# Wk read as plain rows and turned on TensorE at the start of a fused attention and gated-MLP layer

## The chip, the cores and the metric

The kernel runs on one core of a Trainium2 chip. The time is device microseconds of one execution, given as the median of several runs. A second figure is the span of the profiled execution, from its first to its last instruction. TensorE (PE) multiplies matrices into PSUM; VectorE (DVE), ScalarE (ACT) and GpSimd (POOL) do the rest of the arithmetic; SyncE (SP) and ACT issue the transfers (DMA), each through a queue of its own.

## The reference, cut to what matters

x is 2048 x 640, in bf16. The layer has 32 heads of 20 features.

```python
def _A_ref(x, wqkv, w_phi, wo):                 # x: layer-normed rows
    qkv = x @ wqkv                              # 640 -> 3 * 640, split into q, k, v of 32 heads
    pq = einsum("bhsd,hdf->bhsf", q, w_phi)     # a 20 x 20 map per head
    pk = einsum("bhsd,hdf->bhsf", k, w_phi)
    phi_q = concatenate([softmax(pq), softmax(-pq)])
    phi_k = concatenate([softmax(pk), softmax(-pk)])
    kv = einsum("bhsf,bhsd->bhfd", phi_k, v)    # summed over all rows
    z  = einsum("bhsf->bhf", phi_k)
    num = einsum("bhqf,bhfd->bhqd", phi_q, kv)
    den = einsum("bhqf,bhf->bhq", phi_q, z) + 1e-6
    return (num / den) @ wo
h  = x + _A_ref(layernorm(x), wqkv, w_phi, wo)
h2 = h + ((n @ w_gate) * (n @ w_up)) @ w_down   # n = layernorm(h), 640 -> 1536 -> 640
```

## The kernel before, in words

The 2048 rows are cut into 16 tiles of 128 (t = 0 to 15), the 640 features into 5 chunks of 128. The kernel writes its work down as a list of operations with what each reads and writes (`build_graph`). A scheduler, `schedule`, walks that list with a table of planned costs and decides the order on each engine; a program then emits each engine's list with the waits that the reads and writes need. The table `TUNED` (lines 47 to 134) holds, for each operation by name, a key by which the scheduler picks among the operations that are ready, and after a second colon which of several engines does it (0, or nothing, is the first). Every engine works through its list strictly in that order. So the order on the chip comes from `TUNED`, not from the order of the lines.

The stages, by the names that the operations have:

- **Folding the feature map into the weights.** k is needed only as pk, so the kernel multiplies the 20 x 20 maps into Wk once: F1_i, i = 0 to 4 (line 375, function `fold`), six small products for each chunk of 128 rows of Wk. A product takes its stationary operand with the contraction along the partitions, so the fold needs Wk transposed (`wkT`, kept in the buffer `scratch`). Before, wkT comes straight from memory by five transposing loads, wk0 to wk4 (line 282, on SP's queue). The other operand is Phi (line 356: Ph0, Ph1, Ph2), the small maps (w5, from memory) times a 0/1 pattern GL that POOL makes (lines 318 to 337). Fe1_i copies a folded chunk from PSUM to `Wp` (line 237, a helper `copy` used by all evacuations). The same is done for Wq later (F0_i, with transposing loads wqt).
- **Layer norm of x.** x tiles arrive by plain loads (line 272, names x0, x1, x2, x4 and so on; x2 brings tiles 2 and 3, x4 tiles 4 and 5, x6 tiles 6 and 7). Per tile DVE computes statistics (L1s, lines 392 and 393; L1a, line 395), ACT the reciprocal deviation in two steps (L1l and L1e, lines 400 and 403), and DVE or ACT the normed tile xn (lines 428 and 426).
- **Turning x.** Tiles 0 to 3 are transposed on TensorE against an identity matrix, xt0 to xt3 (line 437, five transposes of 128 columns each), and copied to `xnT` by xte0 to xte3 (line 237). Tiles 4 to 15 are turned by transposing transfers from SP (line 446).
- **K and V of each tile** (line 459): V_t from the weights loaded by wv0, wv2, wv4 (line 272), K_t from the folded Wk. Ten products of 320 columns each, evacuated as Ve_t and as two exponentials Kx (line 480); then sums (line 483), reciprocal, scaling on POOL (line 488), and the product KV_t (line 497) that adds up kv and z over the tiles. For tiles 0 and 1 the ten products are five operations of two each, K0_0 to K0_4 and so on, so that each can start when its chunk of weights is there.
- **Q** (line 518), the numerator (551), normalising, the output product with Wo (594), a second layer norm, the gated MLP (636 and 655) and the result (667, 669). The change touches these only through the order.

At the start, before any data is there, TensorE multiplies zeros: 14 products of 512 columns, warm0 to warm13 (line 347). Their result is not used.

The graph of before lists the start of the queues in this form:

```python
xload("sp", 0, 1, -100)
for i in range(NC):
    G.op("sp", "wk%d" % i, lambda e, i=i: e.dma_start_transpose(
        out=T["wkT"][:, :, P * i:P * (i + 1)],
        in_=T["A_wqkv"][P * i:P * (i + 1), D:2 * D]), 1.22, 2.6, [], [wkt_b[i]], key=-99 + i, dma=-1)
xload("act", 1, 2, -95, also=["sp"])
```

With the keys of before SP issues: x0, w5, wk1, wv4, wk2, wk0, x6, wk3, x4, wk4, x8; ACT issues x1, wv0, x2, wv2. TensorE's order is: 14 zero products, xt1, xt0, V1_0, V1_1, F1_1, then sixteen products of V0 and V1, F1_0, F1_2, xt3, xt2, F1_3, K1 and K0, F1_4 and so on.

Of the kernel before, what the change touches and what calls it, by code (L numbers as in the profile page):

```python
# [59 lines left out]
xn9:29.307 xt9:29.987 xn10:29.235:1 xt10:31.207 xn11:36.578:1 xt11:40.017 xn12:43.657:1 xt12:45.087 xn13:42.944:1 xt13:43.867 xn14:45.139 xt14:46.307  # L60
xn15:46.099 xt15:47.527 V0_0:8.987 V0_1:10.074 V0_2:10.345 V0_3:10.617 V0_4:10.889 Ve0:11.43 K0_0:13.51 K0_1:13.782 K0_2:14.054 K0_3:14.325 K0_4:17.085
Kx0_0:18.422 Kx0_1:20.292 Ks0:21.347 Kr0:24.047 Kn0:25.766 KV0:29.582 V1_0:8.129 V1_1:8.4 V1_2:9.259 V1_3:9.53 V1_4:9.802 Ve1:10.344:1 K1_0:12.887
K1_1:13.159 K1_2:14.912 K1_3:15.184 K1_4:16.814 Kx1_0:17.799 Kx1_1:19.045 Ks1:19.927 Kr1:22.767 Kn1:23.407 KV1:31.616 V2:18.715 Ve2:21.539 K2:17.357
Kx2_0:19.669 Kx2_1:20.915 Ks2:25.437 Kr2:28.387 Kn2:29.085 KV2:32.292 V3:15.455 Ve3:17.455:1 K3:20.074 Kx3_0:22.162 Kx3_1:22.995 Ks3:29.807 Kr3:32.047
Kn3:33.803 KV3:37.043 V4:21.432 Ve4:23.619 K4:22.79 Kx4_0:24.419 Kx4_1:25.252 Ks4:26.967 Kr4:28.847 Kn4:31.444 KV4:37.719 V5:32.968 Ve5:34.597
K5:30.258 Kx5_0:32.562 Kx5_1:33.396 Ks5:36.747 Kr5:38.987 Kn5:39.627 KV5:42.47 V6:26.865 Ve6:28.494 K6:28.224 Kx6_0:30.528 Kx6_1:31.361 Ks6:34.257
Kr6:36.177 Kn6:36.817 KV6:43.146 V7:25.507 Ve7:27.552 K7:24.149 Kx7_0:25.875 Kx7_1:26.709 Ks7:39.557 Kr7:42.507 Kn7:43.22 KV7:46.854 V8:41.112
Ve8:42.967:1 K8:39.754 Kx8_0:41.487 Kx8_1:42.32 Ks8:43.719 Kr8:45.639 Kn8:46.279 KV8:48.888 V9:35.685 Ve9:37.915 K9:34.327 Kx9_0:35.955 Kx9_1:37.292
Ks9:41.087 Kr9:46.599 Kn9:48.638 KV9:52.281 V10:38.395 Ve10:40.024 K10:44.137 Kx10_0:45.766 Kx10_1:46.599 Ks10:47.432 Kr10:50.309 Kn10:50.997
KV10:55.674 V11:54.315 Ve11:55.944:1 K11:45.496 Kx11_0:47.222 Kx11_1:48.056 Ks11:48.889 Kr11:50.769 Kn11:53.356 KV11:60.74 V12:57.708 Ve12:59.336  # L70
K12:49.564 Kx12_0:51.193 Kx12_1:52.026 Ks12:53.506 Kr12:55.106 Kn12:58.074 KV12:61.416 V13:50.923 Ve13:52.649 K13:47.53 Kx13_0:49.158 Kx13_1:49.992
Ks13:51.229 Kr13:52.829 Kn13:55.715 KV13:62.722 V14:56.35 Ve14:58.115:1 K14:52.957 Kx14_0:54.585 Kx14_1:55.419 Ks14:56.695 Kr14:58.867 Kn14:60.433
KV14:63.398 V15:64.389 Ve15:66.017:1 K15:59.066 Kx15_0:60.695 Kx15_1:61.528 Ks15:62.361 Kr15:63.961 Kn15:64.601 KV15:68.985 KVe0:69.931 KVe1:70.541
KVe2:71.151 F0_0:60.425 Fe0_0:61.01:1 F0_1:62.407 Fe0_1:63.3 F0_2:62.092 Fe0_2:62.677 F0_3:43.822 Fe0_3:44.407 F0_4:64.074 Fe0_4:64.659 Q0_0:66.826
Qx0_0_0:68.692 Qx0_0_1:68.175 Q0_1:65.747 Qx0_1_0:67.096 Qx0_1_1:67.613 Q0_2:70.74 Qx0_2_0:72.089 Qx0_2_1:72.606 Q0_3:67.905 Qx0_3_0:69.255
Qx0_3_1:69.771 Q0_4:69.661 Qx0_4_0:71.526 Qx0_4_1:71.01 Q1_0:73.933 Qx1_0_0:75.799 Qx1_0_1:75.282 Q1_1:90.247 Qx1_1_0:91.596 Qx1_1_1:92.113 Q1_2:75.012
Qx1_2_0:76.878 Qx1_2_1:76.361 Q1_3:79.676 Qx1_3_0:81.541 Qx1_3_1:81.025 Q1_4:89.168 Qx1_4_0:90.517 Qx1_4_1:91.034 Q2_0:77.172 Qx2_0_0:79.038
Qx2_0_1:78.521 Q2_1:78.596 Qx2_1_0:79.946 Qx2_1_1:80.462 Q2_2:92.751 Qx2_2_0:94.616 Qx2_2_1:94.1 Q2_3:87.744 Qx2_3_0:89.61 Qx2_3_1:89.093 Q2_4:84.961
Qx2_4_0:86.827 Qx2_4_1:86.311 Q3_0:76.093 Qx3_0_0:77.442 Qx3_0_1:77.959 Q3_1:80.755 Qx3_1_0:82.104 Qx3_1_1:82.621 Q3_2:71.819 Qx3_2_0:73.168
Qx3_2_1:73.685 Q3_3:82.524 Qx3_3_0:83.873 Qx3_3_1:84.39 Q3_4:91.326 Qx3_4_0:92.676 Qx3_4_1:93.192 wd0:96.76 wd1:95.06 wd2:94.1 wd3:94.58 N0_1:73.588  # L80
N0_0:72.898 sr0:74.203 rho0:74.693 A0:75.063 B0:76.093 dd0:77.123 rd0:77.513 o0:77.993:1 oT0:78.905 O0:83.603 h0:85.231 L2s0:86.833 L2a0:87.863
L2v0:88.153 L2r0:90.306 hc0:88.153 hT0:89.076 N1_1:78.251 N1_0:73.243 sr1:78.866 rho1:79.356 A1:79.726 B1:80.756 dd1:81.786 rd1:82.176 o1:82.656:1
oT1:83.568 O1:86.386 h1:88.014 L2s1:89.066 L2a1:90.196 L2v1:90.517 L2r1:91.976 hc1:90.626:1 hT1:91.887 N2_1:88.823 N2_0:86.041 sr2:89.886 rho2:90.436
A2:91.126 B2:92.156 dd2:93.186 rd2:93.576 o2:94.056 oT2:95.54 O2:102.227 h2:103.856 L2s2:104.817 L2a2:105.937 L2v2:107.388 L2r2:107.816 hc2:106.399:1
# [131 lines left out]
def mm_c(*ns):  # L216
    return sum(max(0.028, n / 2400.0 + 0.0025) for n in ns)
# [798 lines left out]
```

## Time and profile before

| | |
|---|---|
| median of 5 runs | 283.04 us (282.42 to 283.19) |
| the profiled execution | 283.04 us, span 281.3 us |
| instructions | 4981 |
| granted TensorE clock | 1.000 over the span |
| transfers | 21.98 MB, mean 78 GB/s |

How to read the profile: busy time is the time in which an engine has an instruction in it. A group of instructions of one line is shown with its start, its busy time, what it writes and reads, how many they are, and in brackets how long the engine was idle before and who released it. "PE" is the product on TensorE, "PEld" the loading of its stationary operand, which runs beside it. "SPq" and "ACTq" are issues of transfers. The chain of waits follows the work that ended last back to the start, at each step to what released it.

The busy tenths of TensorE over 40 slices of 7 us:

```profile
PE   6799999999999999999999999999999999999996
```

### The profile page before, as it was taken

Reading aid. Unit: us, or ns where it says so; the run is one execution under the profiler, and the core shown is the slowest. Engines: PE = TensorE matmul, PEld = TensorE weight load, DVE = VectorE, ACT = ScalarE, POOL = GpSimd, SP = SyncE. Lnnn points to the kernel's source line nnn. Section 1 sums busy time; section 2 is a strip of 40 time slices with the busy share of each in tenths; the row PEclk is TensorE's granted clock in tenths of the full one; section 3 lists DMA queues with packets and bytes.
Section 4 is the critical chain, followed back from the end, with each engine's and each line's share of the span. In section 5 each row is a group of like instructions: output and inputs, shape, how many; then the busy total and the mean of one; then the engine's idle time right before and its main releaser. Section 6 shows DMA issues by size and latency. Waiting matters only on the chain.

```text
span 281.3 us, 4981 instructions
## 1 busy us (share of the span) xinstructions
PE 274.0 (97%) x2038; PEld 181.6 (65%) x2054; DVE 181.1 (64%) x370; ACT 102.0 (36%) x182; POOL 60.9 (22%) x77
## 2 busy tenths in 40 slices
PE   6799999999999999999999999999999999999996
PEld 2577878787556689775455664456677454667884
DVE  4799998964488779898577880338793144343242
ACT  2598768545795742113123012211201023230210
POOL 6015997993001222222001000001200000000000
DMA  7937943891012593155202131000236001000002
GB/s 151 265 79 156 154 102 75 249 393 73 0 23 26 121 273 75 26 117 68 51 0 49 23 77 42 0 24 3 50 78 106 24 0 26 1 2 23 29 23 67
DMA packets 46151, 21.98 MB, mean 78 GB/s; under 512 B 37936, under 2 KB 44848, under 8 KB 46128
## 3 DMA queue, kind: packets, MB, share of 16 engines
q1 hardware_dynamic: 45168, 20.52, 32.5%
q10 hardware_dynamic: 960, 1.15, 1.6%
q8 instruction: 16, 0.26, 0.4%
q14 instruction: 7, 0.06, 0.1%
HBM read 10.18 MB, written 2.62 MB: 46 GB/s over the span
## 4 chain that ended last, share of the span: by engine, by line
PE 95%; DMA 3%; issue 0%; SPq 0%; DVE 0%; DVEq 0%
PE ps L636 37%; PE ps L655 19%; PE ps L459 15%; PE ps L594 8%; PE ps L518 8%; PE ps L551 4%; PE ps L497 4%; DMA scratch<-in_A_wqkv_dram 3%; PE ps L375 1%; SPq L272 0%; PE ps L437 0%; DVE Wp L667 0%; DVEq L954 0%
## 5 line engine op out<-in xcount | busy, mean ns | idle before, releaser
L636 PE MATMUL ps<-xnT,Wgu 128*128 128x512 bf16 (+1 forms) x588 | 105.7, 335 | 0.6
L636 PEld LDWEIGHTS ps<-xnT,Wgu 128*128 128x128 bf16 x600 | 58.3, 98 | 43.0 <-DVE ev L644 0.4
L641 ACT ACTIVATE scratch<-ps 128x512 bf16<-128x512 f32 (+1 forms) x60 | 30.6, 511 | 110.6 <-PE ps L636 107.0
L644 DVE TENSOR_TENSOR ev<-ps,scratch 128x512 bf16<-128x512 f32 (+1 forms) x60 | 33.3, 575 | 36.3 <-PE ps L636 19.5
L655 PE MATMUL ps<-Wp,ev 128*128 128x320 bf16 (+2 forms) x396 | 54.0, 295 | 0.0
L655 PEld LDWEIGHTS ps<-Wp,ev 128*128 128x128 bf16 x396 | 38.1, 98 | 14.1
L459 PE MATMUL ps<-Wp,xnT 128*128 128x320 bf16 x320 | 45.6, 299 | 0.4 <-ACT xnT L237 0.4
L488 POOL TENSOR_TENSOR ev<-ev,SR 128x1280 bf16<-128x1280 bf16 x16 | 37.3, 2356 | 8.3 <-DVE SR L486 8.1
L459 PEld LDWEIGHTS ps<-Wp,xnT 128*128 128x128 bf16 x320 | 30.7, 98 | 11.8 <-issue 0.5
L667 DVE SCALAR_TENSOR_TENSOR Wp<-ps,rs,x_all 128x640 bf16<-128x640 f32 (+3 forms) x18 | 14.6, 809 | 25.4 <-PE ps L655 25.2
L583 POOL TENSOR_TENSOR scratch<-scratch,sm 128x640 bf16<-128x640 f32 x10 | 12.7, 1271 | 57.4 <-DVE sm L580 43.6
L527 ACT ACTIVATE eqT<-ps 128x512 bf16<-128x512 f32 x40 | 21.6, 595 | 7.0 <-PE ps L518 7.0
L594 PE MATMUL ps<-Wo,scratch 128*128 128x320 bf16 x160 | 24.2, 299 | 0.0
L483 DVE TENSOR_REDUCE SR<-ev 128x64 f32<-128x1280 bf16 x16 | 23.4, 1475 | 0.7 <-ACT ev L480 0.5
L480 ACT ACTIVATE ev<-ps 128x640 bf16<-128x640 f32 x32 | 20.8, 705 | 7.3 <-PE ps L459 5.9
L608 POOL TENSOR_SCALAR ln<-mv 128x1 f32<-128x1 f32 x16 | 3.3, 209 | 89.0 <-DVE mv L607 77.4
L518 PE MATMUL ps<-xnT,Wp 128*128 128x512 bf16 x96 | 22.3, 379 | 0.2
L598 DVE TENSOR_TENSOR x_all<-ps,x_all 128x640 bf16<-128x640 f32 x16 | 13.2, 822 | 13.0 <-PE ps L594 13.0
L594 PEld LDWEIGHTS ps<-Wo,scratch 128*128 128x128 bf16 x160 | 15.5, 98 | 6.4
L617 ACT ACTIVATE xn<-x_all,mv 128x640 bf16<-128x640 bf16 x9 | 7.4, 825 | 26.1 <-DVE mv L607 26.0
L518 PEld LDWEIGHTS ps<-xnT,Wp 128*128 128x128 bf16 x100 | 9.6, 98 | 9.9 <-DVE KVm L504 0.2
L551 PE MATMUL ps<-KVm,eqT 128*128 128x154 bf16 (+1 forms) x192 | 15.4, 221 | 0.0
(53 smaller groups left out, 202.4 us busy)
## 6 DMA issues: line engine op xcount, KB each, us to landing
out_dram<-Wp SPq DMA_DIRECT2D x15, 160.0 KB, 1.8
x_all<-in_A_x_dram SPq DMA_DIRECT2D x6, 320.0 KB, 3.5
Wgu<-in_B_w_up_dram SPq DMA_DIRECT2D x5, 384.0 KB, 10.1
Wgu<-in_B_w_gate_dram SPq DMA_DIRECT2D x5, 384.0 KB, 6.8
Wp<-in_B_w_down_dram SPq DMA_DIRECT2D x4, 480.0 KB, 5.4
Wp<-in_A_wqkv_dram ACTq DMA_DIRECT2D x2, 320.0 KB, 6.7
Wo<-in_A_wo_dram SPq DMA_DIRECT2D x1, 480.0 KB, 8.5
xnT<-xn SPq DMA_TRANSPOSE x28, 2.6
```

What stands on the lines that cost most here:

```text
L459: ins = e.matmul(pb(b, hb)[:, 0:320], lhsT=T["xnT"][:, NC - 1 - c, P * t:P * (t + 1)], rhs=T["Wp"][:, kind, c, 320 * hb:320 * (hb + 1)], s ...
L480: G.op("act", "Kx%d_%d" % (t, s), lambda e, s=s, b=b, ek=ek: e.activation(out=T["ek"][:, ek.slots[0], s, :].rearrange("p (b n) -> p b n", ...
L483: G.op("dve", "Ks%d" % t, lambda e, ek=ek, sr=sr: e.tensor_reduce(out=T["SR"][:, sr.slots[0], 0, :], in_=T["ek"][:, ek.slots[0], :, :].rea ...
L488: G.op("pool", "Kn%d" % t, lambda e, ek=ek, sr=sr: e.tensor_tensor(out=T["ek"][:, ek.slots[0], :, :].rearrange("p s (h f) -> p (s h) f", f ...
L518: ins = e.matmul(pb(b)[:, 0:n], lhsT=T["Wp"][:, 0, i, P * c:P * (c + 1)], rhs=T["xnT"][:, NC - 1 - i, o0:o0 + n], start=(i == 0), stop=(i ...
L527: G.op("act", "Qx%d_%d_%d" % (q, c, s), lambda e, s=s, c=c, o0=o0, n=n, b=b: e.activation(out=T["eqT"][:, s, c, o0:o0 + n], in_=pb(b)[:, 0 ...
L551: ins = e.matmul(pb(b, y)[:, 22 * h0:22 * (h0 + j1 - j0)], lhsT=T["eqT"][:, s, c, P * t:P * (t + 1)], rhs=T["KVm"][:, OFF[s, c] + j0:OFF[s ...
L594: ins = e.matmul(pb(b, hb)[:, 0:320], lhsT=T["oT"][:, oT.slots[0], c, :], rhs=T["Wo"][:, c, 320 * hb:320 * (hb + 1)], start=(c == 0), stop ...
L636: ins = e.matmul(pb(b)[:, 0:n], lhsT=T["Wgu"][:, gu, c, P * ft:P * (ft + 1)], rhs=T["xnT"][:, NC - 1 - c, o0:o0 + n], start=(c == 0), stop ...
L641: G.op("act", "g%d_%d" % (bi, ft), lambda e, pg=pg, gt=gt, n=n: e.activation(out=T["gt"][:, gt.slots[0], 0:n], in_=pb(pg)[:, 0:n], func=AF ...
L644: o_ = G.op("dve", "u%d_%d" % (bi, ft), lambda e, pu=pu, gt=gt, hh=hh, ft=ft, n=n: e.tensor_tensor(out=T["hh"][:, hh.slots[0], ft, 0:n], i ...
L655: ins = e.matmul(pb(b, hb)[:, 0:w], lhsT=T["hh"][:, hh.slots[0], ft, P * tt:P * (tt + 1)], rhs=T["Wd"][:, ft, c0 + w * hb:c0 + w * (hb + 1 ...
```

## The change: what it does

1. Wk is loaded as plain rows into a new view `wkn` of the scratch buffer: wk0 (rows of chunks 0 and 1), wk2 (chunks 2 and 3), wk4 (chunk 4). Each may go on SP's or on ACT's queue.
2. Each of the five chunks is transposed on TensorE, WT0 to WT4: five transposes of 128 columns against the identity, into one PSUM bank; WTe0 to WTe4 copy the bank to `wkT`. Nothing else that reads `wkT` is changed.
3. The planner's rate for plain loads is written anew, and the whole table `TUNED` is replaced, so the order of every engine is another.

The diff, without the rest of the table:

```diff
-x0:0.7 wk0:4.58 wk1:1.66 wk2:3.36 wk3:6.28 wk4:7.98 x1:0.7 wv0:1.18 wv2:2.14 wv4:2.88:1 x2:1.66 x4:7.5 x6:5.8 w5:1.18 x8:9.2 x10:19.229 x12:26.289
...
+x0:0.7 wk0:1.18:1 wk2:1.66:1 wk4:2.14 x1:0.7 wv0:2.14 wv2:2.62:1 wv4:3.1:1 x2:1.66:1 x4:3.58 x6:2.62:1 w5:1.18 x8:4.06 x10:22.303 x12:22.783 x14:19.383
...
+    wkn_b = [Buf("wkn%d" % i) for i in range(NC)]
     wkt_b = [Buf("wkt%d" % i) for i in range(NC)]
...
     xload("sp", 0, 1, -100)
-    for i in range(NC):
-        G.op("sp", "wk%d" % i, lambda e, i=i: e.dma_start_transpose(
-            out=T["wkT"][:, :, P * i:P * (i + 1)],
-            in_=T["A_wqkv"][P * i:P * (i + 1), D:2 * D]), 1.22, 2.6, [], [wkt_b[i]], key=-99 + i, dma=-1)
+    for n_, (a, b_) in enumerate(((0, 2), (2, 4), (4, 5))):
+        dma("sp", "wk%d" % a, lambda a=a, b_=b_: T["wkn"][:, a:b_, :],
+            lambda a=a, b_=b_: T["A_wqkv"][P * a:P * b_, D:2 * D].rearrange("(c p) n -> p c n", p=P), 164 * (b_ - a),
+            wkn_b[a:b_], key=-99 + n_, also=["act"])
...
+    for i in range(NC):
+        b = Buf("pwt%d" % i, "psum")
+        def wt(e, i=i, b=b):
+            for c in range(NC):
+                ins = e.transpose(out=pb(b).bitcast(BF16)[:, P * c:P * (c + 1)], in_=T["wkn"][:, i, P * c:P * (c + 1)],
+                                  identity=T["ident"][:, :])
+            return ins
+        G.op("pe", "WT%d" % i, wt, mm_c(*[P] * NC), LT, [wkn_b[i], id_b], [b], -90 + i)
+        evac("WTe%d" % i, lambda e, eng, i=i, b=b: copy(
+            e, eng, T["wkT"][:, :, P * i:P * (i + 1)], pb(b).bitcast(BF16)[:, 0:D].rearrange("p (c n) -> p c n", c=NC)),
+             640, [b], [wkt_b[i]], -90 + i, i % 2, 320)
...
-                bw += o.dma / (190.0 if bw < 6.2 else 368.0)
+                bw += o.dma / (300.0 if bw < 4.5 else 200.0 if bw < 7.5 else 368.0)
...
-        sc = sb([P, max(nsc, 2 * NC * D)], BF16, "scratch")
+        sc = sb([P, max(nsc, 3 * NC * D)], BF16, "scratch")
...
+        T["wkn"] = sc[:, 2 * NC * D:3 * NC * D].rearrange("p (c n) -> p c n", c=NC)
```

The order that the new table gives at the start:

- SP issues x0, w5, x2, wk4, wv2, wv4, x4, x8, and then the first transposing transfers of x tiles. ACT issues x1, wk0, wk2, wv0, x6.
- TensorE: nine zero products, WT1, WT0, five zero products, F1_1, F1_0, WT2, xt0, xt1, WT3, F1_2, K0_0 and K0_1, F1_3, V1_0 and K0_2, WT4, V1_1, K0_3, V0_0 and V0_1, F1_4, the rest of V1, of V0, xt2, K0_4, xt3, the first of K1, K2, V2, V3 and so on.
- ACT: two L1l, WTe1, two L1e, Fe1_1, Fe1_0, xte1, Fe1_2, Fe1_3, WTe4, L1l and L1e of tiles 2 and 3, Fe1_4.
- DVE: the statistics of tiles 1 and 0, Ph1 and Ph2, WTe0, xn0 and xn1, WTe2, xte0, WTe3, the statistics of tiles 2 and 3, those of tiles 6 and 7, then xn2 and xn3.
- POOL: the constant of `va` first, the identity, then the pattern GL, eps, Ph0.

Over the rest of the kernel the operations are the same, in another order; POOL scales fewer of the tiles' numerators (line 583) and DVE more.

## The prediction

> **What bounds the kernel now.** I read the page's busy table first, then the chain of waits in order of time, then TensorE's timeline, then the transfers of the first 15 us.
>
> ```profile
> PE 274.0 (97%) x2038; PEld 181.6 (65%) x2054; DVE 181.1 (64%) x370; ACT 102.0 (36%) x182; POOL 60.9 (22%) x77
> ...
> 1.71 8.43 DMA scratch<-in_A_wqkv_dram
> 10.15 0.05 issue
> 10.19 0.49 PE ps L375 x6
> ...
> 269.09 9.82 PE ps L655 x84
> 278.92 0.03 issue
> ```
>
> The chain is TensorE's own work from 10.19 us to 278.92; nothing but breaks of 0.05 us stands between its pieces. Before 10.19 it is one transfer, a transposing load of Wk (scratch is where it lands), issued at 1.71 and on chip at 10.15. So the change can gain only ahead of 10.19, and whatever it adds to TensorE counts in full.
>
> ```profile
> 1.24 4.53 PE L347 MATMUL ps<-zero 128*128 128x512 bf16 x14 [1.24 <-DVE zero L342]
> 7.00 0.97 PE L437 MATMUL ps<-ident,xn 128*128 128x128 bf16 x10 [1.23 <-DVE xn L428]
> 8.34 0.70 PE L459 MATMUL ps<-Wp,xnT 128*128 128x320 bf16 x4 [0.37 <-ACT xnT L237]
> 10.19 0.49 PE L375 MATMUL ps<-Phi,scratch 128*128 128x140 bf16 x6 [1.15 <-DMA scratch<-in_A_wqkv_dram]
> 10.52 2.33 PE L459 MATMUL ps<-Wp,xnT 128*128 128x320 bf16 x16
> ```
>
> TensorE's start: the zero products, the turns of x tiles 0 and 1, four V products, and then the wait for Wk (releasers in brackets). A burst's recorded end carries a tail that the next instruction would hide: a 320-column product takes 0.298 but ten take 1.36, so the tail is 0.16. The array really stands idle 1.23 + 0.16, 0.37 + 0.16 and 1.15 + 0.16, with 0.22 between the two x turns and 0.10 more at 13.6: together 3.55 us.
>
> ```profile
> Wp<-in_A_wqkv_dram ACTq DMA_DIRECT2D x1, 320.0 KB, 5.0
> ...
> scratch<-in_A_wqkv_dram SPq DMA_TRANSPOSE x1, 8.4
> ...
> x_all<-in_A_x_dram ACTq DMA_DIRECT2D x1, 160.0 KB, 3.1
> ```
>
> Three of the first loads, from issue to landing: the second load of ACT's queue (wv0, issued at 1.25) lands at 6.25, the first transposing load of SP's queue at 10.15, x tile 1 at 3.93.
>
> ```profile
> 2.00:4.00 2.00, 2.00 (x6) 0.76 (x5) 0.08 (x1) 0.08 (x1) 1.94 (x9) 1.00 0.95 260
> 4.00:6.00 2.00, 1.77 (x8) 0.59 (x6) 1.84 (x6) 0.26 (x2) 1.40 (x3) 1.00 1.23 232
> 6.00:8.00 2.00, 0.91 (x10) 0.56 (x10) 1.49 (x4) 0.95 (x5) 0.14 (x1) 1.00 0.93 143
> 8.00:10.00 2.00, 0.70 (x4) 0.32 (x4) 1.90 (x6) 0.79 (x2) 0.00 (x0) 1.00 1.33 227
> 11.00:14.00 3.00, 3.00 (x36) 2.39 (x35) 2.19 (x5) 1.92 (x5) 0.00 (x0) 1.00 1.15 325
> ```
>
> Stretches of time: from and to, length, busy time of each engine, then the granted clock (1.00 throughout), the DMA share and GB/s. The rate falls while plain and transposing loads share the engines and recovers to 325.
>
> The profiled execution took 283.04 us, 1.74 around its span of 281.3, and is itself the median of the five runs. The sum is made against it.
>
> **The change part by part.**
>
> *Wk's route.* Five transposing loads leave SP's queue; their issues held it 1.30 + 3.56 + 2.77 + 1.20 = 8.8 us (the two in the middle are one row). Three plain loads of 320, 320 and 160 KB come in: wk0 second and wk2 third on ACT's queue, wk4 fourth on SP's. ACT now issues five loads of about 0.5 us, to about 3.4; its first computing comes at 5.74, so these issues cost nothing. SP now issues x2, wk4, wv2, wv4, x4, x8 one behind the other.
>
> When does wk0 land? Low end: x1's landing 3.93 plus 320 KB at the full 325 GB/s, 4.95. High end: 6.25, where wv0 landed from the same place with the same bytes. By 4.0 the row of 260 GB/s gives 0.52 MB, of which x0, x1 and w5 are 0.35, so 0.17 of wk0's 0.33 MB is in; the other 0.16 MB gets half of 260 GB/s beside x2, 1.2 us. I take 5.3, with 0.1 for the slowest engine. It lies nearer the low end because the transposing loads, beside which wv0's last bytes crept, are gone.
>
> The Trainium skill, DMA: Bandwidth & Descriptors, section Latency and other measured facts, gives a DMA transpose an effective 261 GB/s. By that figure (an estimate from that page) the five Wk tiles would be 3.1 us of transfer against 2.5 at 325 GB/s, Wk would come only some 0.6 us sooner, and after the added transposes the change would lose about 0.9. The row of 8.4 us to landing for one tile speaks against using it here, and the sum goes by the row.
>
> *Added on TensorE.* 25 transposes of 128 columns. Five for x take 0.28 to 0.29 (weight loads, five in 0.28), so 25 take 1.45, all on the path. Nothing is removed: zero products, folds and x turns keep their number.
>
> *Fourteen zero products, split 9 and 5.* One is 0.216 at full clock (14 in 4.53; the last six weight loads in 1.18), so nine end at 4.53, not 5.61. The five others stand behind the first ten transposes and cost 1.08 there; they are no new work, and they cover the evacuation of these transposes (0.70 on ACT). The pause 4.53 to 5.35 is shorter than the 1.39 after which before's transposes still ran 0.28 per five.
>
> *The evacuations.* Five copies of a turned Wk tile: two on ACT (0.70 each by the x copies), three on VectorE, which takes two x copies as well. Such a VectorE copy is not in the trace: between 0.56 (xn, two in 1.12) and 0.83 (the CAST of 640 f32); I take 0.6, since it reads bf16 like the former. What is queued behind: on ACT the two L1e that make rs stand behind WTe1, so rs0 comes at 5.74 + 0.48 + 0.70 + 0.3 = 7.2 and not 6.4, and xn0 and xn1 on VectorE wait for it (7.25 to 8.4). VectorE also takes two of the three Phi products (Ph1, Ph2: 0.27 by size, 0.44), 5.84 to 6.5, ahead of WTe0. TensorE then goes: WT1, WT0 5.35 to 5.93, zero products to 7.01, folds 1 and 0 to 7.65, WT2, xt0 to 8.23, xt1 (waits 0.2 for xn1), WT3, fold 2, K0 (waits 0.3 for xte0), fold 3. Waits 0.1 with the shorter steps, 1.1 with 0.83 per copy; I take 0.4.
>
> *POOL.* The memset of va (1.23) goes first and the identity is made early, by about 3: both before 5.3, no cost. glx, kv1 and one Phi product still end by about 6.5, ahead of the first fold at 7.0.
>
> *x tiles 6 and 7.* x6 is now fifth on ACT's queue, and VectorE has their statistics ahead of xn2 and xn3. Behind that wait stand xn2, the turn xt2 on TensorE, and everything after it. From x6's landing: two pairs of statistics 1.6, aggregate 0.1, xn2 0.56, 2.3 in all. TensorE arrives at xt2 after 1.45 + 1.08 + five folds of 0.32 + 0.58 + 28 products of 0.136 = 8.5 us of work: 5.35 + 8.5 + 0.4 = 14.2. So x6 must land by 11.9. If the two queues are served alike, 2.97 MB must move by then; 0.52 by 4.0, the rest at 325 GB/s is in at 11.5. Ends: 232 GB/s (the row 4 to 6) gives 14.6 and a wait of 2.7; 390 GB/s would give 10.3 (98 to 100 us has that rate). I take 11.5, cost 0, because no transposing load of Wk runs beside them any more.
>
> *K ahead of V in tile 0, and the new order of the other 265 us.* The same products in another order; before shows no wait over 0.05 after 14 us with VectorE 64% and ACT 36% busy. The tail behind the last product (278.92 to 281.3) keeps its form: 128 columns last. I cost both at 0; if the cover is gone, it shows as a wait on TensorE.
>
> Sum: + 1.45 (transposes) + 0.82 (idle 4.53 to 5.35) + 0.4 (waits) − 3.55 (idle before) = −0.88. 283.04 − 0.9 = **282.2**.
>
> **Rivals.**
> A. Forecast, 282.2; its own range 281.6 to 282.5 (wk0 at 4.95 and waits of 0.1 give −1.5, but the first fold still needs WTe1 at 6.9, so no more than −1.4).
> B. Wk is read otherwise but not sooner: wk0 lands at 6.25 as wv0 did. The idle is 1.77: 1.45 + 1.77 + 0.4 − 3.55 = +0.07, 283.1. For it: same place, same bytes. Against: the 143 GB/s of 6 to 8 us fell in the transposing loads' time.
> C. Slower: x6's landing becomes the bound through VectorE's order. Each us past 11.9 costs one; from 13.4 on the change loses more than 0.2%. With 14.6 the time is 284.9. For it: in before the fourth load of ACT's queue took 8.3 us, and x6 is fifth. Against: these rates held transposing loads.
> D. The new order holds a wait later on, of about the gain: 283.0. Against: 36% of VectorE is free.
>
> **How the numbers follow.** A 0.52, B 0.22, C 0.18, D 0.08. Of A nearly all is faster by over 0.2% (0.57 us, about what this kernel's measurement can tell from no change). B and D are mostly no change; some of each falls on either side. Faster 0.55, same 0.25, slower 0.20. The range 281.6 to 284.2 leaves out the low tip of A and the worst of C.
>
> **What would show it.** Transposes of scratch tiles on TensorE near 5.3, no wait on a Wk transfer later; idle ahead of them about 0.8; the folds near 7.0; steady work from there, last product near 278.0. Wrong if wk0 lands after 6, if the line of the x turns shows a wait on VectorE near 14, or if a wait over 0.3 stands behind 20 us.

## The result, and the profile after

| | median | runs |
|---|---|---|
| before | 282.93 us | 80 (281.85 to 285.56) |
| the changed kernel | 284.35 us | 43 (282.71 to 286.46) |
| ratio | 1.0046 | 95% interval 1.0033 to 1.0059 |

The change makes the kernel slower, by 1.3 us by the ratio and 1.4 between the medians. The forecast was 282.2. The profiled execution took 284.58 us, 1.78 around its span of 282.8; the granted clock is 1.00 over the span. The ratios leave out three slow executions of the experiments, all with a lowered clock (E1 286.33 us, E10 419.18, E12 291.49).

Line numbers move by up to 13: zero products L348, transposes of Wk L369, folds L388, products K and V L472, products KV L510. First the page: the busy row and the shares of the chain.

```profile
PE 275.6 (97%) x2064; PEld 183.0 (65%) x2079; DVE 183.8 (65%) x371; ACT 109.8 (39%) x191; POOL 56.2 (20%) x72
...
PE 84%; DVE 5%; DMA 5%; ACT 3%; SPq 1%; issue 1%; DVEq 0%
```

TensorE is busy 1.6 us longer, about the 25 transposes. But the chain, which before was TensorE from 10.19 us to the end, now goes through other engines. These are its pieces in order of time (start, length, what), some left out:

```profile
24.22 4.05 DMA x_all<-in_A_x_dram
...
28.30 0.49 DVE st L405
...
30.97 0.31 ACT ln L413
...
31.51 0.59 ACT ev L493
...
33.64 2.89 PE ps L472 x20
...
38.15 1.27 SPq L301
...
39.47 4.87 DMA scratch<-in_A_wqkv_dram
```

TensorE's timeline says what these two detours cost. The releaser and the idle time ahead of a burst stand in brackets.

```profile
1.24 3.86 PE L348 MATMUL ps<-zero 128*128 128x512 bf16 x9 [1.24 <-DVE zero L343]
6.49 0.73 PE L369 MATMUL ps<-ident,scratch 128*128 128x128 bf16 x10 [1.39 <-DMA scratch<-in_A_wqkv_dram]
7.05 1.24 PE L348 MATMUL ps<-zero 128*128 128x512 bf16 x5
8.13 0.80 PE L388 MATMUL ps<-Phi,scratch 128*128 128x140 bf16 x12
...
33.64 4.24 PE L472 MATMUL ps<-Wp,xnT 128*128 128x320 bf16 x30 [0.69 <-ACT ev L493]
...
44.69 0.48 PE L388 MATMUL ps<-Phi,scratch 128*128 128x140 bf16 x6 [0.69 <-DMA scratch<-in_A_wqkv_dram]
```

The start went as described: the transposes begin at 6.49 where before waited for Wk until 10.19, and from there TensorE stands idle nowhere until 33. Then come two waits of 0.69 (0.85 each with the tail of the product before). The first: x10, which brings x tiles 10 and 11, stands on SP's queue behind the transposing transfer of tile 6, the load x14, and the transfers of tiles 4 and 5. SP's issues:

```profile
19.67 1.30 SPq L459 DMA_TRANSPOSE xnT<-xn  x1
21.02 0.57 SPq L273 DMA_DIRECT2D x_all<-in_A_x_dram  x1
21.64 2.54 SPq L459 DMA_TRANSPOSE xnT<-xn  x2
24.22 1.12 SPq L273 DMA_DIRECT2D x_all<-in_A_x_dram  x2
```

SP has nothing to issue from 4.92 on until the normed tile 6 is there at 19.67, and then works through these without a pause. x10 is issued at 24.22 and lands at 28.28; VectorE's statistics wait for it, ACT's L1l8 (the reciprocal deviation of tiles 8 to 11) waits for VectorE, and behind L1l8 in ACT's list stand exponentials of K, whose PSUM banks TensorE needs. The second: wqt2 and wqt3 stand on the same queue behind the transposing transfers of tiles 9, 10 and 8, are issued from 38.15 on, and the fold F0_3 waits for them.

The last product is at 280.41 (278.92 before): + 1.49.

The loads of the start, in the transfers of the first 15 us, then the stretches of time with their GB/s at the end of each line:

```profile
scratch<-in_A_wqkv_dram ACTq DMA_DIRECT2D x2, 320.0 KB, 5.8
Wp<-in_A_wqkv_dram ACTq DMA_DIRECT2D x1, 320.0 KB, 7.6
x_all<-in_A_x_dram ACTq DMA_DIRECT2D x1, 320.0 KB, 8.8
```

```profile
4.00:6.00 2.00, 1.10 (x3) 0.15 (x1) 1.97 (x7) 0.15 (x1) 0.49 (x4) 1.00 1.03 347
6.00:8.00 2.00, 1.51 (x15) 1.05 (x16) 1.65 (x4) 1.21 (x5) 1.33 (x2) 1.00 1.06 375
8.00:10.00 2.00, 2.00 (x36) 1.88 (x35) 1.67 (x4) 1.35 (x3) 0.00 (x0) 1.00 1.08 370
```

The dip to 143 GB/s of before is gone, and x6, issued at 2.85, is there after 8.8 us, at 11.62. Still wk0, issued at 1.25, is only complete at 6.44.

### The profile page after: what moved, and what is told of

Its sections match the earlier page's. It is cut to its first block, busy times and chain, and to the rows that moved or that the text cites. A ratio compares the mean times of both kernels' runs of the same rounds, so it can differ in the third digit from the quotient of the medians.

```text
span 282.8 us, 5021 instructions
## 1 busy us (share of the span) xinstructions
PE 275.6 (97%) x2064; PEld 183.0 (65%) x2079; DVE 183.8 (65%) x371; ACT 109.8 (39%) x191; POOL 56.2 (20%) x72
## 4 chain that ended last, share of the span: by engine, by line
PE 84%; DVE 5%; DMA 5%; ACT 3%; SPq 1%; issue 1%; DVEq 0%
PE ps L649 37%; PE ps L668 18%; PE ps L607 8%; PE ps L531 7%; PE ps L472 7%; PE ps L564 4%; DMA scratch<-in_A_wqkv_dram 4%; PE ps L510 2%; DVE st L406 2%; DMA x_all<-in_A_x_dram 1%; DVE st L405 1%; ACT eqT L540 1%; SPq L459 1%; ACT ev L493 1%; PE ps L388 1%
## 5 line engine op out<-in xcount | busy, mean ns | idle before, releaser
L472 PE MATMUL ps<-Wp,xnT 128*128 128x320 bf16 x320 | 46.3, 299 | 0.7 <-ACT ev L493 0.7
L472 PEld LDWEIGHTS ps<-Wp,xnT 128*128 128x128 bf16 x320 | 30.4, 98 | 12.2 <-issue 0.9
L630 ACT ACTIVATE xn<-x_all,mv 128x640 bf16<-128x640 bf16 x13 | 10.6, 826 | 36.6 <-DVE mv L620 36.6
L564 PE MATMUL ps<-KVm,eqT 128*128 128x154 bf16 (+1 forms) x192 | 14.5, 221 | 0.0
L596 POOL TENSOR_TENSOR scratch<-scratch,sm 128x640 bf16<-128x640 f32 x6 | 7.6, 1271 | 34.8 <-DVE sm L593 34.8
```

Of the source, the lines that this page charges most:

```text
L472: ins = e.matmul(pb(b, hb)[:, 0:320], lhsT=T["xnT"][:, NC - 1 - c, P * t:P * (t + 1)], rhs=T["Wp"][:, kind, c, 320 * hb:320 * (hb + 1)], s ...
L564: ins = e.matmul(pb(b, y)[:, 22 * h0:22 * (h0 + j1 - j0)], lhsT=T["eqT"][:, s, c, P * t:P * (t + 1)], rhs=T["KVm"][:, OFF[s, c] + j0:OFF[s ...
```

## The experiments

Theory after the first reading: (1) the two later waits come from the order on SP's queue; (2) the rest is the late landing of wk0; (3) the transposes are paid in full. The rival: something else behind the start takes the gain. A helper puts named operations behind another one in an engine's finished list; nothing is planned anew.

One mark serves to compare profiles: the start of the first product KV_0. In the new order the work ahead of it is always the same, and without later waits the last product comes 249.3 us after it (so in eleven of the profiles below). In the profile of before the last product at 278.92 stands for a mark of 29.6. In the profile of the changed kernel the mark is 29.38, and from the first transpose at 6.49 to it TensorE has 22.89 us of work without a break.

### E1 and E2: the loads that came late, issued early

```diff
 order, _ = schedule(G)
+move(order, 'sp', ['x10', 'x12', 'x14'], 'x8')            # E1 and E2
+move(order, 'sp', ['wqt4', 'wqt2', 'wqt3'], 'wqt1')       # E2 only
```

> The changed kernel with one thing moved: the loads x10, x12 and x14 are issued on SP right behind x8, and no longer behind waiting transposes. Theory (two waits of TensorE, at 33.6 and 44.7 us, cost 0.69 us plus a tail of 0.16 each, and the first begins with x10 and x12 landing at 28.3): the wait at 33.6 is gone; 0.85 us less than the changed kernel, 0.16% over the kernel before in place of 0.46%; if the second wait has the same root (xt11 ahead of the last Wq transposes), it goes too and the time is 0.14% below the kernel before. Rival (these waits are slack, the end is set by TensorE's added work): no change, 0.46% over.

> As the run with early x loads, and besides the transposing loads wqt4, wqt2 and wqt3 are issued right behind wqt1. Theory: neither wait is left, TensorE stands only ahead of the first Wk transposes; 1.7 us less than the changed kernel, 282.5 where before has 282.9. Rival (the wait is set by something else, the transposes of x tiles 9 and 10 that now stand behind three more transposing loads): a wait of about 1 us near 34, no gain over the run with early x loads.

E1: median 283.22, ratio to before 1.0014 (0.9984 to 1.0044). E2: 282.71, ratio 1.0005 (0.999 to 1.0021). TensorE's timeline of E1:

```profile
22.52 6.96 PE L472 MATMUL ps<-Wp,xnT 128*128 128x320 bf16 x50 [0.28 <-DMA xnT<-xn]
...
32.73 4.24 PE L472 MATMUL ps<-Wp,xnT 128*128 128x320 bf16 x30
...
43.16 0.48 PE L388 MATMUL ps<-Phi,scratch 128*128 128x140 bf16 x6
```

Both later waits are gone, the second already in E1. E1's interval is too wide to tell it from the changed kernel or from before; E2 is level with before. So the loss against before comes from the places of these loads on SP's queue. But nothing is gained over before either. In E2's profile TensorE waits for wk2; that execution, of 283.90, was the slowest of the twelve:

```profile
5.39 0.73 PE L369 MATMUL ps<-ident,scratch 128*128 128x128 bf16 x10 [0.26 <-DMA scratch<-in_A_wqkv_dram]
...
9.41 0.45 PE L369 MATMUL ps<-ident,scratch 128*128 128x128 bf16 x5 [1.57 <-DMA scratch<-in_A_wqkv_dram]
```

### E3: the transposes twice

E2, with each of the 25 transposes done a second time.

```diff
-            for c in range(NC):
+            for c in list(range(NC)) * 2:
                 ins = e.transpose(out=pb(b)..., in_=T["wkn"][:, i, P * c:P * (c + 1)], ...)
```

> As the run with early x and Wq loads, and each of the 25 transposes of Wk is made twice. Theory (they lie on TensorE's path in full): 1.45 us more than that run. Rival (they fill time in which TensorE would wait for evacuations or VectorE): the first ten cost 0.6 and the others little, 0.6 us more or less.

Median 284.76, 2.05 above E2; ratio to before 1.009 (1.0062 to 1.0119). In its timeline:

```profile
6.53 1.29 PE L369 MATMUL ps<-ident,scratch 128*128 128x128 bf16 x20 [1.82 <-DMA scratch<-in_A_wqkv_dram]
...
30.78 0.84 PE L510 MATMUL ps<-ev 128*128 128x147 bf16 x12
```

From the first transpose to the first KV product it is 24.25, against 22.89: 1.36 more, near the 25 x 0.056 = 1.4 that these cost by themselves. They are hidden nowhere. The other 0.6 of the difference in the medians is not explained; this profile has a late wk0 and one wait of 0.46 near 127 us.

### E4: nine zero products

E2, without the five zero products between the transposes and the folds (`warm9` to `warm13` taken out of the list).

> As the run with early x and Wq loads, and without the last five zero products, those between WT0 and fold 1; nine are left. Theory (they only cover the evacuations of the first two turned tiles; fold 1 can start about 7.75 when WTe1 has landed, not at 8.13): 0.4 us less than that run at most, and none if xn0 and xn1 on VectorE are what TensorE then waits for. Rival (they keep the clock up): the granted clock falls or products near 8 us take twice as long, and the run is slower.

Median 283.10, ratio 1.0026 (1.0007 to 1.0045); nothing is won by leaving them out.

```profile
7.08 0.81 PE L388 MATMUL ps<-Phi,scratch 128*128 128x140 bf16 x12 [0.68 <-ACT scratch L237]
8.46 0.45 PE L369 MATMUL ps<-ident,scratch 128*128 128x128 bf16 x5 [0.57 <-DMA scratch<-in_A_wqkv_dram]
```

Where they stood, TensorE now waits for the evacuation of WT1, and then for wk2. So the five did lie beside other work. Part of the rival shows in the other executions: two of E4's twelve, and three of E6's twelve, which leaves out the same five, have a granted clock of 0.993 or 0.994 over the span (283.91 to 284.88 us), and of the other 215 executions of the new order only four have one under 0.995. So the five products seem to help to keep the clock up; the profiles of E4 and E6 have it at 1.00, and how it falls is not shown.

### The changed kernel again

The changed kernel as it is, for a second profile.

> The changed kernel, unchanged, for a second profile. Theory: the two later waits (for x10's statistics near 33.6 us, for wqt near 44.7 us, 0.69 us each in the first profile) come from the order and are there again, 0.4 to 1.0 us each, while wk0's landing (6.44) and wk2's (8.07) differ by up to 1 us from the first profile. Rival: the two waits are an accident of that execution, as the landings are, and are gone or under 0.2.

Median 283.94, ratio 1.0043 (1.0019 to 1.0068). The theory missed in part:

```profile
5.27 0.73 PE L369 MATMUL ps<-ident,scratch 128*128 128x128 bf16 x10 [0.61 <-DMA scratch<-in_A_wqkv_dram]
...
9.44 0.45 PE L369 MATMUL ps<-ident,scratch 128*128 128x128 bf16 x5 [1.71 <-DMA scratch<-in_A_wqkv_dram]
...
33.67 4.24 PE L472 MATMUL ps<-Wp,xnT 128*128 128x320 bf16 x30
...
44.20 0.48 PE L388 MATMUL ps<-Phi,scratch 128*128 128x140 bf16 x6 [0.17 <-ACT ev L237]
```

The wait near 33.6 is not there, that at the fold F0_3 is down to 0.17 and ended by ACT, not by a load. Here wk0 came at 5.2, and wk2 at 9.4 instead of 8.07, so TensorE reached the KV mark at 30.26, 0.88 later than in the first profile. Yet the products of L472 start at 33.67, where the first profile, with its wait, has 33.64. x10 was issued 0.65 later here (24.87), since VectorE's list had moved with TensorE's, and landed at 28.15 all the same, 3.3 us after its issue instead of 4.05. So the later waits are there or not according to how late the start was and how long x10 took: the two sources of loss don't simply add up, and over ten executions the kernel is as slow as in the first comparison. Here the last product comes at 279.92, 1.00 after that of before: 0.66 of it is the late mark, 0.33 the wait at F0_3 with its tail. The late mark is the work of wk2 and not of wk0, so point 2 of the theory doesn't hold for this execution.

### E5 and E6: wk2 on the other queue

E2, with x2 and wk2 exchanged: SP issues x0, w5, wk2, wk4 and so on, ACT x1, wk0, x2, wv0, x6. E6 leaves out the five late zero products as well.

```diff
 order, _ = schedule(G)
+swap(order, 'x2', 'wk2')
```

> E2 with one exchange: wk2 (chunks 2 and 3 of Wk) is third on SP's queue, behind w5, and x2 third on ACT's, behind wk0. In E2 wk2 landed at 9.36 us and WT2 waited 1.57; in the other profiles of the new order it landed at 8.07 to 8.5 and WT2 waited 0.5. Theory 'wk2 is late because it is queued behind wk0 on the same queue': it lands beside wk0, at 6 to 7.3, WT2 waits for nothing, and the time is 0.5 to 1.5 us below E2's, so 281.3 to 282.4 where the kernel before is 282.8. Rival 'all the bytes of the first 8 us set it, whatever the queue': wk2 lands at 8 or later, or wk0 is pushed back by what wk2 gains; no change from E2, 282.5 to 283.

> E5 without the five late zero products. If wk2 is there by 7, the first folds start when WTe1 has been copied, about 0.4 us earlier than with the five zero products in front of them: 0.3 to 0.5 us below E5. Rival: nothing, because the next thing TensorE needs (WTe0, wk2 or xn0 and xn1 on VectorE) does not come earlier; within 0.2 us of E5.

E5: 283.06, ratio 1.000 (0.9974 to 1.0027). E6: 283.82, ratio 1.0036 (1.0011 to 1.0061). E5's timeline:

```profile
5.44 0.73 PE L369 MATMUL ps<-ident,scratch 128*128 128x128 bf16 x10 [0.42 <-DMA scratch<-in_A_wqkv_dram]
...
22.61 6.96 PE L472 MATMUL ps<-Wp,xnT 128*128 128x320 bf16 x50 [0.47 <-DMA xnT<-xn]
```

As theory said, wk2 is no longer waited for, though it landed at 7.88 and not at 6 to 7.3. The time did not follow: TensorE waits for the turned tile 6 at 22.61 instead. The chain of E5 leads back from there over xn6 on ACT and VectorE's statistics to x6, which landed at 11.96. In E6 the missing zero products turn into waits for WTe0 on VectorE (0.96) and for wv0 (0.74), and the wait for tile 6 remains.

### E7: the same early loads in the kernel before

The two moves of E2, made in the kernel before.

> The kernel before, with x10, x12 and x14 and with wqt4, wqt2 and wqt3 issued as early on SP's queue as in E2. Theory: before has no wait on TensorE behind 14 us, so nothing changes: within 0.3 us of before. Rival: loads issued early are of use in either kernel, and E2's gain over the changed kernel is no repair of what the new order did: 0.5 us or more below before.

Median 286.57, ratio 1.0137 (1.0087 to 1.0187): neither of the two, but clearly slower.

```profile
11.23 0.53 PE L375 MATMUL ps<-Phi,scratch 128*128 128x140 bf16 x6 [2.19 <-DMA scratch<-in_A_wqkv_dram]
11.56 4.01 PE L459 MATMUL ps<-Wp,xnT 128*128 128x320 bf16 x16
...
34.03 2.21 PE L459 MATMUL ps<-Wp,xnT 128*128 128x320 bf16 x15 [2.94 <-DMA xnT<-xn]
```

```profile
24.34 6.53 SPq L300 DMA_TRANSPOSE scratch<-in_A_wqkv_dram  x5
30.91 14.90 SPq L446 DMA_TRANSPOSE xnT<-xn  x6
```

The five transposing loads of Wq, now in one row from 24.34 on, stand ahead of the transfer that turns x tile 6, and TensorE waits 2.94 for it. The wait of 2.19 is not the moves' doing: the first Wk load landed at 11.18, 1.03 later than in before, and the moved plain loads were issued only from 14.01 on. The six executions fall into two groups, 285.19 to 285.57 with a granted clock of 1.000 and 287.57 to 288.85 with 0.994; the profile is of the second. So E2's gain over the changed kernel repairs that kernel's order; early loads are no gain as such.

### E8: no wait for Wk at all

E2, but the transposes read x tiles 0 and 1, on chip by 4.02 us, and wait for these instead of wk0, wk2 and wk4.

```diff
-                ins = e.transpose(out=pb(b)..., in_=T["wkn"][:, i, P * c:P * (c + 1)], ...)
+                ins = e.transpose(out=pb(b)..., in_=T["x"][:, i % 2, P * c:P * (c + 1)], ...)
```

> E2, but the 25 transposes read x tiles 0 and 1 (on chip by 4.02 us) where they read Wk; Wk is still loaded, so the traffic is the same, and every copy, fold and product is done, on other numbers. This leaves out what the computation takes from Wk. Theory 'the landings of wk0 and wk2 are all that keeps E2 from its gain': in E2's profile they cost 0.26 and 1.57 us, in the other profiles of the new order together 0.9 to 2.3; without them the time is 281.2 to 281.8, about 1 us or more below the kernel before. Rival 'the next limit stands right behind': the turn of x tile 2 waits for x6 (landing near 11.7, 2.3 us of VectorE behind it) near 14 us, or the products of tile 6 wait near 22.6 for its turned tile, and what is saved at the start is idle there; 282.3 or more.

Median 282.54, ratio 1.0003 (0.999 to 1.0015). By its time the rival holds. The profile, of 283.96 and the slowest of the twelve, shows one more wait than it named:

```profile
11.27 0.72 PE L472 MATMUL ps<-Wp,xnT 128*128 128x320 bf16 x4 [1.27 <-DMA Wp<-in_A_wqkv_dram]
...
23.71 6.96 PE L472 MATMUL ps<-Wp,xnT 128*128 128x320 bf16 x50 [0.56 <-DMA xnT<-xn]
```

TensorE begins its transposes at 4.89 and then waits 1.27 for the V weights wv0, and 0.56 for tile 6 (x6 landed at 12.97). With the landing of Wk out of the way altogether, the median is that of before. How long these two waits are in an execution near the median is not shown.

### E9 to E11: tile 6 earlier, work while wk2 is on its way

E9 is E5 with `xn6` ahead of the exponential `Kx2_0` on ACT. E10 is E2 with WT2 behind xt0 and xt1 on TensorE, and WTe2 behind xte0 on VectorE. E11 has both moves, on E2.

```diff
+move(order, 'act', ['Kx2_0'], 'xn6')       # E9, E11
+move(order, 'pe', ['WT2'], 'xt1')          # E10, E11
+move(order, 'dve', ['WTe2'], 'xte0')       # E10, E11
```

> E5, with one exchange on ACT: xn6 stands ahead of the exponential Kx2_0 (0.70 us), so that the transposing transfer of tile 6 is issued near 18.4 and not 19.09. In E5's profile TensorE waited 0.47 us for that tile at 22.61. Theory 'VectorE's and ACT's work on x tiles 4 to 7 is the next limit': the wait is gone and the time is 0.3 to 0.6 us below E5, 282.4 to 282.8. Rival: K2's PSUM banks come free 0.7 us later and TensorE waits for these instead, no change from E5.

> E2, with WT2 behind the turns of x tiles 0 and 1 (ten transposes of 128 columns, 0.57 us) and WTe2 behind xte0 on VectorE, so that TensorE has work while wk2 is on its way. Theory: where wk2 lands at 8.1 to 9.4, 0.3 to 0.57 us of the wait at WT2 are covered; 0.2 to 0.5 us below E2 in the same call's terms, 282.2 to 282.6. Rival: the x turns wait for xn1 on VectorE (near 8) in place of it, and nothing is won.

> E10 and E9's exchange on ACT together, on E2's queues. Theory: both waits shrink, 282.0 to 282.5, below the kernel before by 0.2 to 0.7 us. Rival: where wk2 is late, TensorE arrives at tile 6 late enough not to wait, so the exchange on ACT adds nothing to E10.

E9: 282.81, ratio 1.0024 (1.0005 to 1.0044). E10: 283.50, 1.0031 (1.0016 to 1.0045). E11: 282.97, 1.0014 (1.0001 to 1.0028). None is below before. In E9's profile x6 came at 12.67, so tile 6 was turned no earlier than in E5 and its chain still leads through it. In E10 and E11 WT2 waits for nothing, but the next fold waits 0.31 for WTe2, which now stands behind xte0. E11's profile has the earliest KV mark of all, 29.09; that execution took 282.57.

### E12 to E17: the x tiles untied

E12 (on E5) and E13 (on E10): VectorE norms tiles 2 and 3 ahead of the statistics of tiles 6 and 7, ACT computes the reciprocal deviation of tiles 6 and 7 apart from that of 4 and 5, and xn6 follows the copy of xt3. E14 is E12 with the transposes reading x tiles 0 and 1 as in E8.

```diff
-LNG = [[0], [1], [2, 3], [4, 5, 6, 7], ...]
+LNG = [[0], [1], [2, 3], [4, 5], [6, 7], ...]
...
+# VectorE: L1a3, xn2, xn3, L1s6, L1s7, L1a6, L1a7, L1s4, xte2, ...
+# ACT:     Kx0_0, L1l6, L1e6, xte3, xn6, Kx0_1, ...
```

> E5, with the x tiles' work untied: on VectorE xn2 and xn3 stand ahead of the statistics of tiles 6 and 7 (so the turn of tile 2 no longer waits for x6), the aggregate of tile 7 follows that of tile 6, the reciprocal deviation of tiles 6 and 7 is computed apart from that of 4 and 5 (two more small activations, 0.5 us on ACT), and xn6 follows the copy of xt3, so that tile 6 is turned some 1.5 us earlier. Theory 'x6's landing and the work on tiles 4 to 7 are the limit behind the landings of Wk': the waits near 14 and 22.6 us (0.19 and 0.47 in E5's profile, 0.6 in E8's) are gone, the first KV product starts at 28.3 to 28.8 (29.41 in E5) and the time is 282.0 to 282.4. Rival: another wait of the first 30 us takes their place, or the shift comes back behind 30 us; 282.7 or more, as E5.

> The same untying on E10 (wk2 second Wk load on ACT's queue, WT2 behind the turns of x tiles 0 and 1). Theory: as E12, with WT2's lateness and the 0.31 us at the next fold left; 282.2 to 282.7, 0.5 us or more below E10. Rival: no change from E10, 283.2 or more.

> E12, but the 25 transposes read x tiles 0 and 1 in place of Wk, as in E8 (what the computation takes from Wk is left out, the loads stay). The floor of this design: if Wk's landing and the x tiles' work are the two limits, both are out of the way and the first KV product starts at 27.6 to 28.2, the time is 281.4 to 282.0. Rival: the V weights wv0 (11.2 us in E8, where V1_0 waited 1.27 for them) or x2 bind next, and it is no better than E12.

E12: 283.83, ratio 1.0031 (1.0011 to 1.0052). E13: 284.09, 1.0053 (1.0029 to 1.0077). E14: 283.11, 1.0013 (0.9996 to 1.003). The three don't answer the question: tile 6 is no longer waited for, but the edit made a wait of its own, the same in all three; in E12:

```profile
17.35 13.09 PE L472 MATMUL ps<-Wp,xnT 128*128 128x320 bf16 x94 [0.65 <-DVE xnT L237]
```

E15, E16 and E17 are E12, E14 and E13 with that copy, xte2, ahead of the statistics of tile 4.

```diff
+move(order, 'dve', ['L1s4'], 'xte2')
```

> E12 with one exchange on VectorE: the copy of turned x tile 2 stands ahead of the statistics of tile 4. In E12, E13 and E14 alike that copy came 0.75 us late by the new order of VectorE and TensorE waited 0.65 for it (0.8 with the tail of the products before), so none of the three told what was asked. Theory 'x6 and the work on tiles 4 to 7 are the limit behind the landings': without that wait the first KV product starts at 29.2 to 29.6 (30.28 in E12) and the time is 282.6 to 283.1: as low as E5, not lower, since wv0, which lands at 10.5 to 11, now holds the start. Rival 'the x tiles alone were the limit': 282.0 to 282.4.

> E14 with the same exchange (what the computation takes from Wk is left out, the loads stay). The floor of this design with neither Wk's landing nor the x tiles in the way: E14 less 0.8, so 282.1 to 282.5, the first KV product at 28.8 to 29.1, with wv0 near 10.5 the only wait left. Rival: something that is not a landing takes it back, 282.8 or more.

> E13 with the same exchange. Theory: E13 less 0.8, 283.1 to 283.4, the first KV product at 29.1 to 29.4. Rival: 282.5 or less, then it beats the kernel before.

E15: 283.46, ratio 1.0018 (0.9997 to 1.0039). E16: 283.20, 1.0005 (0.9988 to 1.0022). E17: 283.76, 1.0041 (1.0019 to 1.0064). All three are above what theory gave, and all three show the same new wait; in E15:

```profile
10.66 0.72 PE L472 MATMUL ps<-Wp,xnT 128*128 128x320 bf16 x4 [0.32 <-DMA Wp<-in_A_wqkv_dram]
...
18.50 11.58 PE L472 MATMUL ps<-Wp,xnT 128*128 128x320 bf16 x84 [0.76 <-ACT ev L493]
```

ACT now does the x tiles' work ahead of the exponentials of K, and TensorE waits for the PSUM banks that these hold. In E16, which waits neither for Wk nor for tile 6, this 0.76 (0.92 with the tail) and a slow start of TensorE (below) are all that its profile shows: from its first transpose to WT2 it is 3.24 us, against 2.29 in the changed kernel. Together they eat the whole gain of that execution. So the rival of E16 holds: it is not only landings.

### What the runs say together

| | waits of TensorE in the profile after 5 us (us, for what) | KV mark | the profiled execution | median | ratio |
|---|---|---|---|---|---|
| changed | 1.39 wk0, 0.69 x10, 0.69 wqt | 29.38 | 284.58 | 284.35 | 1.0046 |
| E2 | 0.26 wk0, 1.57 wk2 | 30.24 | 283.90 | 282.71 | 1.0005 |
| E5 | 0.42 wk0, 0.47 tile 6 | 29.41 | 282.87 | 283.06 | 1.000 |
| E8 | 1.27 wv0, 0.56 tile 6 | 30.51 | 283.96 | 282.54 | 1.0003 |
| E11 | 0.28 wk0, 0.31 WTe2 | 29.09 | 282.57 | 282.97 | 1.0014 |
| E15 | 0.23 wk0, 0.32 wv0, 0.76 K on ACT | 29.92 | 283.40 | 283.46 | 1.0018 |
| E16 | 0.76 K on ACT | 29.83 | 283.29 | 283.20 | 1.0005 |

The waits and the mark belong to one execution each. Those of E2 and E8 were the slowest of their twelve: in both wv0 landed at 11.2 and x6 at 12.9 or later, where the first profile of the changed kernel has 9.88 and 11.62. From the last product to the time it is 4.1 to 4.2 us in these profiles, so the medians of E2 and E8 stand for marks near 29.2 and 29.1 (an estimate), 1.0 and 1.4 earlier than in their rows.

Eighteen profiles of the new order were taken. The first transpose lies between 4.80 and 6.53, the KV mark between 29.09 and 30.51 (E3 with its doubled transposes, 30.78, aside), and 29.6 is what before has. A start at 5.2 with 22.89 of unbroken work would be 28.1. In the profiles each limit that was taken away gave way to another one: wk0, wk2, wv0, x6 with the turn of tile 6, ACT's exponentials. That no order reaches 28.1 is not shown; none of those tried did. No version beats the kernel before.

The stretches of time show why the reserve is so small. First before, then the changed kernel; VectorE's busy time is the third figure after the length, ACT's the fourth.

```profile
12.00:14.00 2.00, 2.00 (x29) 1.68 (x27) 2.00 (x5) 1.10 (x2) 0.00 (x0) 1.00 1.16 324
14.00:20.00 6.00, 6.00 (x56) 4.45 (x53) 6.00 (x20) 5.57 (x11) 0.97 (x4) 1.00 0.23 68
20.00:30.00 10.00, 10.00 (x76) 7.19 (x75) 10.00 (x18) 8.74 (x17) 5.34 (x5) 1.00 0.82 170
```

```profile
12.00:14.00 2.00, 2.00 (x22) 1.51 (x19) 2.00 (x9) 1.59 (x4) 0.00 (x0) 1.00 0.07 22
14.00:20.00 6.00, 6.00 (x53) 4.48 (x51) 6.00 (x16) 5.65 (x11) 0.97 (x4) 1.00 0.00 0
20.00:30.00 10.00, 10.00 (x81) 7.17 (x80) 8.10 (x18) 8.61 (x14) 6.88 (x3) 1.00 1.16 184
```

In before VectorE is busy 18.00 of the 18 us from 12 to 30, ACT 15.41. In the changed kernel VectorE is busy all of the time from 12 to 20; from 20 to 30 it waits 1.71 for x10. That TensorE didn't wait in before because it came late, and VectorE had no time to give, is read from these busy times; no run gave VectorE less to do.

## Why the prediction was wrong

**K ahead of V and the new order at 0: the step that failed.** Rival D had the right mechanism, with a chance of 0.08, and its price was too low. In the profiled execution the new order holds two waits, 2 x 0.85 = 1.70; with the loads that they wait for issued early (E2) the kernel is level with before. The argument against it was that 36% of VectorE is free. That is the average over the whole span. In the stage where the new order has to work, from 12 to 20 us, VectorE was free 0% in both kernels, as the rows above show. The other half of the error: a load on SP's queue was costed as hidden without asking what waits ahead of it. x10 has no wait of its own; the transposing transfer of tile 6 in front of it has, until 19.67, and then come 4.5 us of issues.

**wk0's landing: the term that was mis-sized.** 5.3 was taken; 6.44 was measured in the first profile; in the others in which the transposes waited for it they began between 5.03 (E11) and 6.53 (E3). The transposes began 1.14 later than forecast (6.49 against 5.35). The idle ahead of them grew by less, to 1.39 + 0.16 from 0.82, since the nine zero products also ended later, at 4.94 without the tail instead of 4.53. Rival B's bound of 6.25 was too low as an upper end. What no step named is wk2, which gates WT2 in the same way and came between 8.07 and 9.4 in both profiles of the changed kernel and in E1, E2 and E4. In the second profile its 1.71 is the largest wait.

**The sum, term by term, in the first profile:** −0.88 of the forecast, + 1.14 for the start of the transposes (wk0 at 6.44 against 5.3), − 0.40 for start-up waits that were not there, + 1.70 for the two later waits: + 1.56. Measured + 1.49 in the last product. The sum closes for that execution only. Its terms are not independent: the chain of that profile leads from wk0 over TensorE and VectorE's list to the issue of x10. And E8 shows that even with the term for wk0 at nothing, and no wait for x10, the gain is not there. What takes it in a typical execution stays open: the waits are shown only for the executions that were profiled. Two of the three signs that the prediction named for being wrong came: wk0 after 6, and waits over 0.3 behind 20 us.

**Right:** the transposes, 1.45 and all on the path (E3: 1.36 for 25 more). x6 taken at 11.5, landed 11.62, so rival C fell in that execution, though x6 came at 12.7 to 13.0 in the second profile, in E8 and in E9, past the 11.9 that the prediction asked for. That it landed in time was partly luck. The copy of a turned Wk tile on VectorE, taken at 0.6, took 0.49; the waits of the start, taken at 0.4, were none. The five late zero products cost nothing (E4), and seem to guard the clock, which the prediction didn't have.

**The figure of the skill.** The Trainium skill, DMA: Bandwidth & Descriptors, section Latency and other measured facts, gives a DMA transpose 261 GB/s with a non-contiguous middle dimension and about 350 to 400 GB/s in the contiguous case; the prediction took the first without its condition. By it Wk would have come only some 0.6 us sooner (an estimate). The transposes began at 6.49 and 5.27 in the two profiles of the changed kernel where before got its Wk at 10.15; the row of 8.4 us was the one to go by. That the change loses, as the estimate from the page's figure had it, has another reason.

## What to carry to other kernels

A chain that is all one engine says that the others kept up with its present pace, not that they could with an earlier start: look at the busy time of each feeder in the stage where the work moves to, not at its average. Before a gain at the start is booked, take the first points at which a load or another engine's work must be ready, here wv0 near 11 us, the turned tile 6 near 22.6 and x10 near 28: what is saved ahead of such a point counts only as far as it has slack. And on a queue that issues in order, a plain load stands behind every wait of the transfers in front of it, as x10 did here. Last, a profile is one execution: set its time beside the median before its waits are taken to explain the median.

## What the runs showed of the hardware

**The same load lands at different times.** wk0, issued at 1.25, was complete between 5.0 (E11) and 6.8 us (E14) in the profiles of the new order. In the first profile the trace's records of the 16 transfer engines show 15 of them done with it by 5.59 and the last at 6.44. So an estimate of a landing needs a margin of about a microsecond here.

**TensorE's pace at the start varies, and the rows don't show it.** The same nine zero products took between 3.42 and 4.02 us, with a granted clock of 1.00 in every row. In E16 the pace had not risen by 6.3 us; its chain has:

```profile
5.26 1.07 PE ps L369 x10
6.33 1.48 PE ps L348 x5
```

In the changed kernel's chain the same ten transposes took 0.73 up to the start of the next piece and the five zero products 1.08. The traces' records of the clock begin with 1.00 at 7.01 in E16, at 4.80 in the first profile of the changed kernel and at 3.92 in the second. The rows show 1.00 before that too, where no record lies, and six of the twenty traces, that of before among them, have no record at all: there the clock has to be read from the durations. The Trainium skill, TensorE: Matmul & The Clock Gate, section Part 1 on the clock gate, says that the window by which the clock is released runs freely, so that the number of slow products at the start differs between executions of one kernel; these durations agree with it.

**Behind a wait of 2.19 us the pace was halved, behind shorter ones it was not.** In E7 sixteen products after it took 4.01 us where before took 2.33, and the granted clock is 0.50 from 11.56 to 14.97:

```profile
12.00:14.00 2.00, 2.00 (x10) 1.11 (x8) 0.07 (x1) 0.88 (x3) 0.00 (x0) 0.50 1.15 329
```

After the waits of 1.71 (the changed kernel again) and 1.82 (E3) the records stay at 1.00; E2 has none, but after its wait of 1.57 five transposes took 0.45, as elsewhere. Only three of E7's six executions show the lowered clock, as do 6 of the 150 executions of before that were run beside the experiments (0.994 over the span, 284.88 to 285.71 us). Whether the length of the wait alone decides is not shown.
